# Storing the sums of a weight matrix's quarters from GpSimd's queue, every third step

## The chip, the cores and the metric

The kernel runs on one core of one Trainium2 chip. Its time is the device time of one execution in microseconds (us); a comparison uses the median of several timed runs. Traces come from one profiled execution, whose time is given beside its span. The engines are TensorE (PE, matrix products; PEld is its loading of weights), VectorE (DVE), ScalarE (ACT), GpSimd (POOL) and SyncE (SP, which here only issues DMA transfers, in the order in which they were written down). Each engine works through its own list of instructions in order, and waits where an instruction needs what another engine or a transfer has not delivered.

## The reference, cut to what matters

```
scores = matmul(q, k^T) / sqrt(64)         # 8 batches, 8 heads, 576 tokens, head of 64
keep in each row the scores that are at least its 32nd largest
attn   = softmax of what is kept;  x = matmul(attn, v), heads side by side: (8, 576, 512)
u      = x + real(fft over channels of fft over tokens of x)
un     = (u - mean(u)) / sqrt(var(u) + 1e-6)
out    = u + relu(un @ w1) @ w2            # w1: 512 x 2048, w2: 2048 x 512, all float32
```

## The kernel before

**The order of work.** All instructions are written out in the order wanted, in a loop of steps. A step `i` is one tile of 128 rows of scores (576 columns): a pair of heads has nine tiles, a batch four pairs, so a batch has 36 steps (`PER_BATCH`). In step `i` VectorE finds the 32 largest of each row of tile `i`, four rounds of MAX8 (L425) with MATCH_REPLACE8 (L427) between them, two tiles interleaved. GpSimd then scales the smallest and the largest of them (`bounds`, L434, tile `nt`). One or two steps later the tile is masked: ScalarE computes a penalty from `nt` (L448), GpSimd subtracts it from the scores (`mask`, L451, tile `wk`), ScalarE takes the exponential (L459). For most pairs from the second batch on (`by_dma`) the tile is then transposed by DMA: ScalarE copies it as two planes (L472), SP stores these (L485, L488) and reads them back transposed into `PT` (L506). TensorE multiplies `PT` with `v` (L564), computes the scores of the tile three steps ahead (L401, L386, L371), which ScalarE copies to `S` (L404, L393, L375), and in between works through a queue of units of the previous batch's two layers: the first (`hp`, L966), the second (`cp`, L993, L1032). A table `plan`, filled by `at(step, where, fn)`, holds what is issued at a fixed place of a step. The places that matter here: "pool" and "load2" both stand at the end of a step, behind that step's `bounds`, and "load2", last of all, issues transfers on SP.

**The quarters of the second layer.** From the second batch on a part of the second layer is computed with seven products of half matrices in place of eight (`fast`). It needs four sums of the quarters of `w2`, T1 to T4, which are made once. `w2` lies as 16 blocks of 128 rows; `NK` is 8, and for each `kc` of 0 to 7 the function `parts_of_w2` takes the blocks `kc` and `8 + kc`, each cut into two halves of 256 columns, and makes the four sums on GpSimd by four subtractions of 128 x 256 numbers (L923), two in a call with `half` 0 and two in the next with `half` 1. The four lie in a tile `t` of 128 x 4 x 256 numbers, 512 KB. This tile has one buffer (tag `fold_d`), so the first subtraction of the next `kc` waits until the store of the one before has landed. The store goes into the DRAM tensor `scr` (`w2_parts`; in the profile `w_parts<-w_t`, L925), each partition as four pieces of 1 KB. It is planned for "load2" of the step after the second half, on SP, in line behind everything that SP still has to issue. The program table has a quarter every two steps, from step 50 (`PER_BATCH + 14`): halves in steps 50 and 51, 52 and 53, to 64 and 65. In step 50 SP also stores two of `w2`'s quarters as they are, 1 MB each (L1379). The sums are read back by `bring` (L909) when the second batch's layers are computed.

Steps 36 to 62 are masked by way of DMA transposes, steps 63 to 71, the second batch's last pair, by TensorE (L527). Beside the quarters GpSimd has other work in these steps, two additions of the second layer's result (L1022). Behind the stage the second batch's folds (`fold_ops`) use `fold_d` again, from step 75 on.

Of the kernel before, what the change touches and what calls it, by code (L numbers as in the profile page):

```python
# [73 lines left out]
def kernel(  # L74
# [9 lines left out]
    nc = tc.nc  # L84
# [243 lines left out]
    PER_BATCH = NPB * PER_PAIR  # L328
# [574 lines left out]
    scr = dramp.tile([P, len(OPS), NK, DH], F32, name="w2_parts", tag="w2_parts")  # L903
# [9 lines left out]
    def parts_of_w2(kc, half):  # L913

        if half == 0:
            parts[kc] = batp.tile([P, 4, DH], F32, name=f"w2_t_{kc}", tag="fold_d")
        t, lo, hi = parts[kc], w2[:, kc, :], w2[:, NK + kc, :]
        sums = (
            (T1, lo[:, DH:], lo[:, 0:DH]), (T2, hi[:, DH:], t[:, T1]),
            (T3, hi[:, DH:], lo[:, DH:]), (T4, hi[:, 0:DH], t[:, T2]),  # L920
        )
        for out_, in0, in1 in sums[2 * half:2 * half + 2]:
            nc.gpsimd.tensor_tensor(out=t[:, out_], in0=in0, in1=in1, op=ALU.subtract)  # L923
        if half:
            at(now[0] + 1, "load2", lambda: nc.sync.dma_start(out=scr[:, 0:4, kc, :], in_=t))  # L925

# [377 lines left out]
    def at(step, where, fn, cost=0.0):  # L1306
        plan.setdefault((step, where), []).append(fn)
        costs[step] = costs.get(step, 0.0) + cost
# [63 lines left out]
    for kc in range(NK):  # L1372
        for half in range(2):
            at(
                PER_BATCH + 14 + 2 * kc + half, "pool",
                lambda kc=kc, half=half: parts_of_w2(kc, half),
            )
    for o, place in ((B12, w2_12), (B21, w2_21)):
        at(PER_BATCH + 14, "load2", lambda o=o, place=place: nc.sync.dma_start(  # L1379
            out=scr[:, o], in_=place  # L1380
# [65 lines left out]
    queue, waiting, pending, written, now, out_next = [], [], [], set(), [0], []  # L1446
# [227 lines left out]
```

## Time and profile before

| | us |
|---|---|
| median of 3 timed runs | 1862.91 (1859.79 to 1863.91) |
| the profiled execution | 1856.28 |
| its span, first to last instruction | 1854.5 |
| busy: PE / DVE / ACT / POOL | 1688.5 / 1584.3 / 1294.3 / 912.5 |
| mean granted clock of TensorE | 0.96 |
| the 32 sums L923 on POOL | 319.3 to 417.1 from the span's start |
| the 8 stores L925 on SP, issued | 339.2 to 417.2 |

How to read the profile: a line of a group gives engine, source line, operation, `out<-in` by the program's names, shapes and how often (x). "`A L1 <- B L2: s, n, m`" in the view of waits means that instructions of line L1 on engine A stood idle until something of L2 on B ended: s us in all, n times, m the longest. In a timeline a line gives start, duration, engine, line and operation, and in brackets the idle time just before and what ended it. The view by stretches gives, for a stretch of the span, each engine's busy time with its number of instructions (PE, PEld, DVE, ACT, POOL), the granted clock of TensorE, the DMA engines' mean busy share and GB/s. The chain is the work that ended last, each piece followed back to what released it. Issuing a transfer doesn't count as busy; SPq marks SP's issue of one.

### The profile page before, as it was taken

Reading aid. Unit: us, or ns where it says so; the run is one execution under the profiler, and the core shown is the slowest. Engines: PE = TensorE matmul, PEld = TensorE weight load, DVE = VectorE, ACT = ScalarE, POOL = GpSimd, SP = SyncE. Lnnn points to the kernel's source line nnn. Section 1 sums busy time; section 2 is a strip of 40 time slices with the busy share of each in tenths; the row PEclk is TensorE's granted clock in tenths of the full one; section 3 lists DMA queues with packets and bytes.
Section 4 is the critical chain, followed back from the end, with each engine's and each line's share of the span. In section 5 each row is a group of like instructions: output and inputs, shape, how many; then the busy total and the mean of one; then the engine's idle time right before and its main releaser. Section 6 shows DMA issues by size and latency. Waiting matters only on the chain.

```text
span 1854.5 us, 26992 instructions
## 1 busy us (share of the span) xinstructions
PE 1688.5 (91%) x8134; PEld 1082.4 (58%) x8134; DVE 1584.3 (85%) x3301; ACT 1294.3 (70%) x3104; POOL 912.5 (49%) x1278
## 2 busy tenths in 40 slices
PE   5676699789899898999999999999999999999999
PEld 3343465355465664557565665667565756686677
DVE  7999989889999999999999999999999998944010
ACT  6878658577688778878788778877887778642100
POOL 4768743454753466346543565355634654350012
PEclk8778799899999999999999999999999999999999
DMA  5333115661456954568465945586457845520051
GB/s 168 106 88 114 27 41 148 186 168 38 121 137 158 233 151 123 134 178 222 112 153 146 246 124 137 141 222 171 122 137 180 213 112 140 153 82 7 6 173 57
DMA packets 516576, 249.16 MB, mean 134 GB/s; under 512 B 398288, under 2 KB 506448, under 8 KB 516432
## 3 DMA queue, kind: packets, MB, share of 16 engines
q1 hardware_dynamic: 515664, 247.23, 51.2%
q8 instruction: 65, 1.06, 0.2%
q14 instruction: 79, 0.65, 0.1%
q10 hardware_dynamic: 768, 0.21, 0.0%
HBM read 93.63 MB, written 84.74 MB: 96 GB/s over the span
## 4 chain that ended last, share of the span: by engine, by line
PE 43%; DVE 24%; POOL 11%; ACT 9%; issue 7%; DMA 4%; SPq 1%; POOLq 0%; DVEq 0%; ACTq 0%
PE hp L966 15%; DVE wk L427 11%; DVE m L425 10%; PE o L564 5%; PE cp L993 5%; POOL wk L451 5%; PE cw L1163 4%; PE sp L401 3%; ACT wk L448 2%; PE cv L1163 2%; POOL fg L651 2%; PE yp L755 2%; ACT wk L472 1%; POOL zw L678 1%; PE cp L1032 1%
## 5 line engine op out<-in xcount | busy, mean ns | idle before, releaser
L451 POOL TENSOR_TENSOR wk<-S,wk 128x576 f32<-128x576 f32 x288 | 407.5, 1415 | 485.2 <-ACT wk L448 484.8
L425 DVE MAX8 m<-wk 128x8 f32<-128x576 f32 x864 | 626.4, 749 | 6.1
L966 PE MATMUL hp<-unT,w 128*128 128x256 f32 (+1 forms) x2048 | 526.1, 409 | 5.3 <-ACT hT L970 4.6
L966 PEld LDWEIGHTS hp<-unT,w 128*128 128x128 f32 x2048 | 380.3, 191 | 109.8 <-issue 10.4
L427 DVE MATCH_REPLACE8 wk<-m,wk 128x576 f32<-128x576 f32 x576 | 427.5, 742 | 0.0
L472 ACT COPY wk<-S 128x576 uint16<-128x576 uint16 x468 | 289.6, 670 | 0.0
L448 ACT ACTIVATE wk<-S,nt 128x576 f32<-128x576 f32 x288 | 223.4, 776 | 85.3 <-POOL nt L434 84.0
L993 PE MATMUL cp<-w,hT 128*128 128x512 f32 x512 | 234.9, 599 | 0.0
L970 ACT ACTIVATE hT<-hp 128x320 f32<-128x320 f32 (+1 forms) x256 | 103.3, 411 | 177.2 <-PE hp L966 175.6
L425 DVE MAX8 m<-S 128x8 f32<-128x576 f32 x288 | 213.7, 742 | 15.6 <-ACT S L375 15.6
L459 ACT ACTIVATE S<-wk,nt 128x576 f32<-128x576 f32 x234 | 184.2, 787 | 50.5 <-POOL wk L451 49.2
L427 DVE MATCH_REPLACE8 wk<-m,S 128x576 f32<-128x576 f32 x288 | 213.7, 742 | 0.0
L564 PE MATMUL o<-PT,v 128*64 128x256 f32 (+3 forms) x1440 | 199.3, 421 | 14.5 <-ACT x L627 5.9
L401 PE MATMUL sp<-kT,qT 64*128 64x512 f32 (+1 forms) x528 | 170.4, 673 | 12.2 <-ACT means L1357 5.7
L564 PEld LDWEIGHTS o<-PT,v 128*64 128x64 f32 x1440 | 115.7, 155 | 90.8 <-issue 22.3
L404 ACT COPY S<-sp 128x512 f32<-128x512 f32 (+1 forms) x264 | 141.8, 588 | 27.9 <-PE sp L401 26.9
L993 PEld LDWEIGHTS cp<-w,hT 128*128 128x128 f32 x512 | 93.9, 192 | 90.2 <-issue 89.3
L1108 POOL TENSOR_TENSOR hT<-hT 128x512 f32<-128x512 f32 x64 | 81.2, 1275 | 117.0 <-ACT hT L970 87.9
L434 POOL TENSOR_TENSOR nt<-m,cc 128x2 f32<-128x2 f32 x288 | 60.2, 209 | 155.4 <-DVE m L425 154.8
L1163 PE MATMUL cw<-w,hT 128*128 128x256 f32 x448 | 105.3, 385 | 12.2 <-ACT ct L1133 10.1
L371 PEld LDWEIGHTS sp_t<-kt,qT 128*128 128x128 f32 x320 | 51.0, 194 | 108.9 <-issue 67.6
L1163 PEld LDWEIGHTS cw<-w,hT 128*128 128x128 f32 x448 | 83.1, 191 | 27.9 <-ACT ct L1133 12.5
(160 smaller groups left out, 2129.6 us busy)
## 6 DMA issues: line engine op xcount, KB each, us to landing
planes<-wk SPq DMA_DIRECT2D x208, 288.0 KB, 2.7
w<-w_parts SPq DMA_DIRECT2D x82, 512.0 KB, 4.7
space<-in_moe_w_ch_dram SPq DMA_DIRECT2D x32, 512.0 KB, 3.6
nat<-in_q_dram SPq DMA_DIRECT2D x128, 64.0 KB, 2.3
v<-in_v_dram SPq DMA_DIRECT2D x64, 128.0 KB, 2.9
out_dram<-x SPq DMA_DIRECT2D x32, 256.0 KB, 2.8
nat<-in_k_dram SPq DMA_DIRECT2D x62, 128.0 KB, 3.0
planes<-wk SPq DMA_DIRECT2D x52, 144.0 KB, 2.6
```

The lines of the kernel that those rows point to most:

```text
L401: nc.tensor.matmul(sp[r], lhsT=qT[hd, q_cols], rhs=kT[hd, :], start=True, stop=True)
L404: nc.scalar.copy(out=s_t[r, keys], in_=sp[r])
L425: ops.append(lambda src=src, m8=m8: nc.vector.max(out=m8, in_=src))
L427: ops.append(lambda src=src, m8=m8: nc.vector.match_replace(w, m8, src, NEG))
L448: nc.scalar.activation(out=w, in_=Ssb[i], func=AF.Relu, scale=-FAR, bias=Nt[i][:, 1:2])
L451: nc.gpsimd.tensor_tensor(out=w, in0=Ssb[i], in1=w, op=ALU.subtract)
L459: nc.scalar.activation(out=Ssb[i] if by_dma(i) else w, in_=w, func=AF.Exp, bias=Nt.pop(i)[:, 0:1], accum_out=den_t[pair % 3][:, c:c + 1],)
L472: nc.scalar.copy(out=words[:, half, :], in_=src[:, half, :])
L564: nc.tensor.matmul(o[D * e:D * (e + 1), c0:c1], lhsT=vv[:, c, e, :], rhs=pt[:, NF if c == NF else (NF + 1) * e + c, c0:c1], start=(c == 0) ...
L966: nc.tensor.matmul(hp[:, 0:w], lhsT=w1[:, dt, P * it:P * (it + 1)], rhs=unT[:, dt, 0:w], start=(dt == 0), stop=(dt == NDT - 1),)
L993: nc.tensor.matmul(cp, lhsT=hT[:, it, P * n:P * (n + 1)], rhs=w2[:, it, :], start=(it == 0), stop=(it == NIT - 1),)
L1163: nc.tensor.matmul(dst, lhsT=h()[a][:, kc, :], rhs=rhs_of(kc), start=start and kc == 0, stop=kc == NK - 1, skip_group_check=True,)
```

## The change

Two edits. The store of a quarter is issued by GpSimd itself, right behind the four sums, in the step of the second half; it is no longer planned for the next step on SP. And a quarter is begun every third step, from step 47 on: halves in steps 47 and 48, 50 and 51, to 68 and 69.

```diff
@@ parts_of_w2
         for out_, in0, in1 in sums[2 * half:2 * half + 2]:
             nc.gpsimd.tensor_tensor(out=t[:, out_], in0=in0, in1=in1, op=ALU.subtract)
         if half:
-            at(now[0] + 1, "load2", lambda: nc.sync.dma_start(out=scr[:, 0:4, kc, :], in_=t))
+            nc.gpsimd.dma_start(out=scr[:, 0:4, kc, :], in_=t)
@@ the table of the plan
     for kc in range(NK):
         for half in range(2):
             at(
-                PER_BATCH + 14 + 2 * kc + half, "pool",
+                PER_BATCH + 11 + 3 * kc + half, "pool",
                 lambda kc=kc, half=half: parts_of_w2(kc, half),
             )
```

In the built program the lists of TensorE, VectorE and ScalarE keep their order. On GpSimd the sums stand in other places among the masks, and the eight stores follow their sums, each waiting for the last of them; the next quarter's first sum waits for the store. On SP eight transfers are gone, and the others keep their order.

## The prediction

> **What bounds the kernel now.** The page first: TensorE is busy 91% of the span and VectorE 85%, so neither bounds everywhere, and the change touches one stage only, the quarters of the second layer, which run on GpSimd from 319 to 417 us. So I read that stage by itself. The view by stretches shows it against its neighbours (the columns are busy time and instructions of each engine, granted clock, DMA share, GB/s):
>
> Ahead of the stage:
>
> ```profile
> 300.00:320.00 20.00, 17.11 (x70) 9.09 (x69) 19.76 (x42) 16.17 (x42) 7.02 (x9) 0.91 0.49 134
> ```
>
> In it and behind it:
>
> ```profile
> 340.00:360.00 20.00, 12.40 (x42) 5.38 (x39) 16.47 (x35) 10.07 (x26) 10.18 (x14) 0.74 0.65 182
> 360.00:380.00 20.00, 16.95 (x75) 6.74 (x73) 14.78 (x31) 14.95 (x39) 10.74 (x15) 0.91 0.49 147
> ...
> 420.00:440.00 20.00, 19.54 (x115) 13.10 (x113) 19.76 (x42) 15.85 (x48) 6.25 (x9) 1.00 0.14 31
> ```
>
> Before and after the stage VectorE (third busy figure) works 19.76 of 20 us: its top-k chain sets the pace, 5.09 us from one tile's first MAX8 to the next (320.60, 325.69, 330.77, 335.86). Inside the stage VectorE, TensorE and ScalarE all fall off together, and the granted clock with them. The waits of 316 to 430 us, engine by engine, say why:
>
> ```profile
> POOL w_t L923 <- DMA w_parts<-w_t: 36.4, 7, 11.0
> ```
> ```profile
> DVE m L425 <- ACT S L375: 6.6, 3, 4.3
> DVE rd L591 <- ACT rd L590: 5.4, 2, 2.9
> DVE wk L427 <- POOL w_t L923: 0.9, 1, 0.9
> DVE ct L1052 <- ACT ct L1048: 0.8, 1, 0.8
> ```
>
> GpSimd waits seven times, 36.4 us in all, for the store of the quarter before; VectorE loses 13.7 us in the same stretch, and TensorE 16.3. That the first makes the others is read from the order of work. On GpSimd:
>
> ```profile
> 332.00 0.19 POOL L434 TENSOR_TENSOR nt<-m,cc 128x2 f32<-128x2 f32 x1
> 343.17 0.72 POOL L923 TENSOR_TENSOR w_t<-w 128x256 f32<-128x256 f32 x1 [10.98 <-DMA w_parts<-w_t]
> 343.97 0.72 POOL L923 TENSOR_TENSOR w_t<-w,w_t 128x256 f32<-128x256 f32 x1
> 344.66 1.40 POOL L451 TENSOR_TENSOR wk<-S,wk 128x576 f32<-128x576 f32 x1
> ```
>
> The next tile's mask (L451) stands behind the blocked quarter. ScalarE's exponential at 346.09 has then waited 10.76 us for that mask, and the copies of the scores, which VectorE and TensorE need, stand behind it. The chain of waits of this stage runs the same way, and through SP:
>
> ```profile
> 338.58 0.59 SPq L255
> 339.18 0.04 issue
> 339.22 3.81 DMA w_parts<-w_t
> 343.08 0.09 issue
> 343.17 0.72 POOL w_t L923
> ```
>
> The first quarter's sums were done at 325.8, but its store was issued on SP at 339.22: it is queued there behind transposes, planes and the loads of v. The data then need 3.81 us (over all eight: 2.9 to 3.8). So 13.4 of 17 us were queueing.
>
> **The change, part by part.**
>
> *Removed: the place on SP.* Eight issues of 0.39 to 0.60 us go from SP, and with them the queueing. Otherwise no instruction of TensorE, VectorE or ScalarE changes its place, and SP's other transfers keep their order. On GpSimd the same 32 sums of 0.73 us (23 us) remain.
>
> *Moved: the spacing.* A quarter is made in steps 47+3k and 48+3k instead of 50+2k and 51+2k. Two whole steps, 2 x 5.09 = 10.2 us, now lie between a store's sums and the next quarter's; taking off the 1.45 us of the sums themselves, 8.7 us are left for issue and landing before GpSimd would wait. The first quarter now ends near 310 us (the L434 of step 48 stands at 308.96), ahead of the two 1 MB stores of L1379 at 322, and the last ones, in steps 65 to 69, fall where no sums were before (GpSimd is busy only 6.25 of 20 us from 420 to 440). The last store is issued in step 69; the next user of its buffer, the second batch's folds, comes from step 75. The first reading back of the parts is at 592.5 us. Both are covered.
>
> *Added: eight transfers issued by GpSimd.* The trace has none, so the time c for which one holds GpSimd is bounded by rows. Low end: SP's quickest issue of this very store, 0.39 us. High end: 4.7 us, the median landing of the 512 KB loads of L909, as if GpSimd were held until the data lay there. I take 2.0 us, the slowest issue of such a load on SP (1.99), since it is an issue and not a landing, and GpSimd has to prepare 128 x 4 pieces of 1 KB. What is queued behind it on GpSimd is the next tile's mask (L451) and, through it, ScalarE's exponential. After the undisturbed first quarter's second half GpSimd was idle 1.46 us before that mask (at 327.24). With 2.0 us in that gap the mask is late by 0.54 us, eight times: 4.3 us of lateness. The exchange rate of this stage is 13.7 us of VectorE for 36.4 of GpSimd, 0.38, so at most 1.6 us; as each lateness stands alone and the next two steps have slack, I take half, 0.8. At c = 4.7 it is 3.24 x 8 x 0.38 = 9.8 us, at 0.39 nothing.
>
> A rule speaks against the change. The rows: GpSimd's sums take 718 to 744 ns, each of the 32, with VectorE working 87% of the stage beside them; VectorE's MAX8 and MATCH_REPLACE8 don't hold GpSimd's work up. The Trainium skill, "SBUF — State Buffer", section "SBUF: two separate sides", warns that descriptors written by GpSimd starve while VectorE holds the port pair that the two share, in copies and other two-port modes. If these VectorE instructions held it, a store could wait for VectorE's gaps, and the gain would go; the rows make me think they don't. The skill's "DMA: Bandwidth & Descriptors", section "Latency and other measured facts", gives about 1 us to the first byte on GpSimd's path; with c = 1 nothing would be late and the 0.8 us would drop out.
>
> *The landing.* 2.0 + 3.8 = 5.8 us, within 8.7. Only the second quarter's store, near 326 us, meets the 1 MB stores of L1379 (4.7 and 8.5 us to land): 2.0 + 8.5 - 8.7 = 1.8 us, at 0.38 is 0.7; the next store moves half the bytes, so I take 0.4.
>
> *What is late next.* Of VectorE's 13.7 us, 0.8 (L1052) and 0.15 of L425 follow TensorE's own work: 1.0 us stays. TensorE is busy 97.75 of 114 us at a clock of 0.93, VectorE 99.18: without the stalls both need about 100, and both come out ahead by about the same, so what comes later is earlier by that amount; from 420 us both are above 19.5 of 20 busy.
>
> *Sum:* 13.7 - 1.0 - 0.8 - 0.4 = 11.5 us gained. The profiled execution took 1856.28 us (span 1854.5), so 1844.8 by its measure. It was faster than the three timed runs (1859.79 to 1863.91); against their median, 1862.91, the forecast is **1851.4**. Ends of this case: with c at 4.7, 13.7 - 1.0 - 9.8 - 0.4 = 2.5 gained, 1860.4; if TensorE's 16.3 us come back whole, because it bounds what follows, 1846.6.
>
> **Rivals.**
>
> 1. *The wait goes, and SP's and ScalarE's chain takes its place* (about 6 us gained, 1857). In this stage SP waits 12.1 us in L506 for planes to land and 23.7 in L485 for ScalarE; GpSimd's own store shares the 16 DMA engines with the transposes (share 0.6). If the transposed tiles then come late, TensorE's L564 waits and perhaps half of 11.5 is kept. Against it: at 300 to 320 us the same transposes run at VectorE's full pace, and SP loses eight issues.
>
> 2. *Slower: GpSimd becomes the bound by preparing the transfer.* Three steps last 15.3 us; GpSimd's masks and bounds take 3 x 1.60, the sums 2.92: 7.5 us are free. From c = 7.5 GpSimd sets the pace of the stage, and each store costs c - 7.5. At 7.5 + 13.7/8 = 9.2 us the gain is used up; at 11 us, 8 x 3.5 - 13.7 = 14 us are lost: 1877. [...] Against it: no row of an issue on any engine for a plain transfer exceeds 2 us.
>
> 3. *No change: the store lands too late here too.* If software's transfer through contended DMA engines takes longer than 8.7 us by the 5 us that a wait lasts now (36.4/7), the waits are back in the same place, at three steps: 1863.
>
> **How the numbers follow.** Forecast, within its ends: 0.65. Rival 1, faster too: 0.14. Rival 2: 0.14. Rival 3: 0.07. About 0.2%, 3.7 us, is what a measurement of this kernel can tell from no change; a small part of the forecast's high end falls within it, and part of rival 3 outside, so faster 0.77, same 0.08, slower 0.15. The range runs from 1846 to 1862: it holds the forecast with both ends of c, rival 1 and some of rival 3, and leaves out the slower case and what little lies below.
>
> **What would show it.** Right: no wait of L923 for w_parts, or under 3 us in all; VectorE at 19.5 of 20 in 320 to 420 us; the tile that starts its top-k at 428.13 now starts near 416; MAX8 gaps near 5.09. The distance on GpSimd from the end of a quarter's last sum to the next L451, less ScalarE's release, shows c. Wrong: that distance above 5 us with ScalarE waiting for L451 (rival 2), waits of L923 for a landing (rival 3), waits of L564 for PT (rival 1).

## The result, and the profile after

Over 22 runs each on the same chips the changed kernel takes 1854.51 us (median; 1846.04 to 1860.43), the one before 1860.36 (1856.85 to 1865.70): a ratio of 0.9967, 95% interval 0.9956 to 0.9978, so 5.9 us or 0.33% faster. Its profiled execution took 1850.13 us (span 1848.4), 6.15 less than the profiled one before. The forecast was 11.5 us; the direction and the range held, the size is about half.

The waits of 300 to 430 us in the changed kernel, on GpSimd, VectorE and TensorE:

```profile
POOL w_parts L925 <- POOL w_t L923: 2.1, 7, 0.3
```
```profile
DVE ct L1052 <- ACT ct L1048: 1.0, 1, 1.0
DVE m L425 <- ACT S L375: 0.9, 2, 0.7
```
```profile
PE o L564 <- DMA PT<-planes: 6.4, 1, 6.4
PE o L564 <- ACT x L627: 2.9, 1, 2.9
```

The 36.4 us of L923 for the store are gone, and VectorE's idle time is 1.9 us where it was 13.7. TensorE has a wait in the stage that was not there: 6.4 us for a transposed tile. Before, all of its 16.3 us were waits for ScalarE, these two among them (316 to 430 us):

```profile
PE sp_t L371 <- ACT qT L316: 5.1, 1, 5.1
PE o L564 <- ACT x L627: 3.1, 1, 3.1
```

One quarter's second half on GpSimd, with its store:

```profile
321.65 0.73 POOL L923 TENSOR_TENSOR w_t<-w 128x256 f32<-128x256 f32 x1
322.33 0.73 POOL L923 TENSOR_TENSOR w_t<-w,w_t 128x256 f32<-128x256 f32 x1
323.37 0.79 POOL L925 DMA_DIRECT2D w_parts<-w_t  x1 [0.31 <-POOL w_t L923]
324.18 1.42 POOL L451 TENSOR_TENSOR wk<-S,wk 128x576 f32<-128x576 f32 x1
```

A store holds GpSimd for 0.31 + 0.79 = 1.1 us, and here the mask follows at once. The stretches that carried the stall:

```profile
340.00:360.00 20.00, 13.57 (x48) 6.13 (x46) 19.76 (x42) 12.82 (x33) 10.59 (x14) 0.74 0.85 219
360.00:380.00 20.00, 18.39 (x87) 10.92 (x86) 18.19 (x37) 15.69 (x40) 8.26 (x11) 1.00 0.70 161
```

VectorE now works 19.76 of 20 us from 340 to 360 (16.47 before). TensorE works 13.57 us there, hardly more than the 12.40 before, and now for another reason. The chain of that stretch names it:

```profile
346.25 2.81 DMA planes<-wk
349.06 0.02 issue
349.07 4.50 DMA PT<-planes
353.57 0.25 issue
353.82 4.53 PE o L564 x20
```

and SP's issues show why the planes set out only at 346:

```profile
318.32 1.05 SPq L1379 DMA_DIRECT2D w_parts<-w  x2
319.41 8.24 SPq L506 DMA_TRANSPOSE PT<-planes  x1
327.77 1.23 SPq L488 DMA_DIRECT2D planes<-wk  x2
331.26 1.30 SPq L506 DMA_TRANSPOSE PT<-planes  x1
```

The transpose behind the two 1 MB stores of L1379 takes 8.24 us to be issued, where the others from there to 370 us take 1.3 to 4.0; everything on SP comes later from there.

**Where the time went.** Instructions of VectorE keep their order, so one and the same can be compared: its lead is how much earlier it starts than in the first profile before. Leads in us, worked out from the traces, at MAX8 of a tile; "stage" is the difference between tiles 40 and 88, "behind" between 88 and the last:

```
                                tile 40   tile 88   tile 287   stage   behind
changed kernel                     2.7      13.9       7.1      11.2     -6.8
changed kernel, again (e4)         1.2       8.5      -0.3       7.3     -8.9
spacing alone (e1)                 0.2      11.0       9.1      10.8     -1.9
SP, three steps, same step (e8)    0.2      11.0       4.5      10.8     -6.5
queue alone (e2)                   1.8       9.2       9.7       7.4      0.5
late copies alone (e7)             2.8       6.6       2.4       3.9     -4.2
both edits, late copies (e3)       1.6      19.2      13.9      17.6     -5.4
the same again (e12)               1.8      19.4      10.9      17.6     -8.5
spacing, SP, late copies (e6)      1.2      18.8      19.3      17.6      0.5
the same again (e11)               0.8      18.3      12.5      17.5     -5.8
before, again (e5)                 0.3       0.2       1.0       0.0      0.7
```

So the stage gave what was forecast in one profile and less in the other (2.7 and 1.2 us of lead were there ahead of it, where the two programs don't differ), and then some 7 to 9 us were given back in the 1100 us from there to the last tile, where no instruction differs either. One program's stage varies as well: e10 below, which is the kernel before up to tile 90, took 6.0 us longer in it than the first profile before. Two questions for the runs: what each edit does, and where the second half went.

### The profile page after: what moved, and what is told of

It reads as the page before. It is cut to its first block, busy times and chain, and to the rows that moved or that the text cites. A ratio compares the mean times of both kernels' runs of the same rounds, so it can differ in the third digit from the quotient of the medians.

```text
span 1848.4 us, 26992 instructions
## 1 busy us (share of the span) xinstructions
PE 1686.1 (91%) x8134; PEld 1084.1 (59%) x8134; DVE 1581.0 (86%) x3301; ACT 1294.9 (70%) x3104; POOL 919.5 (50%) x1286
## 3 DMA queue, kind: packets, MB, share of 16 engines
q1 hardware_dynamic: 511440, 243.04, 51.2%
q0 software_dynamic: 1152, 4.19, 0.7%
## 4 chain that ended last, share of the span: by engine, by line
PE 45%; DVE 27%; POOL 9%; issue 8%; ACT 7%; DMA 3%; SPq 0%; POOLq 0%; DVEq 0%; ACTq 0%
PE hp L966 16%; DVE wk L427 12%; DVE m L425 12%; PE cp L993 5%; PE o L564 5%; POOL wk L451 4%; PE sp L401 3%; PE cw L1163 3%; PE cv L1163 2%; ACT wk L448 2%; PE yp L755 2%; POOL fg L651 2%; PE cp L1032 2%; PE mp L816 1%; PE sp_t L371 1%
## 5 line engine op out<-in xcount | busy, mean ns | idle before, releaser
L425 DVE MAX8 m<-S 128x8 f32<-128x576 f32 x288 | 213.7, 742 | 10.3 <-ACT S L375 10.2
L564 PE MATMUL o<-PT,v 128*64 128x256 f32 (+3 forms) x1440 | 198.7, 421 | 22.0 <-DMA PT<-planes 13.0
L401 PE MATMUL sp<-kT,qT 64*128 64x512 f32 (+1 forms) x528 | 168.9, 669 | 9.3 <-ACT means L1357 5.7
L564 PEld LDWEIGHTS o<-PT,v 128*64 128x64 f32 x1440 | 116.0, 155 | 97.8 <-issue 34.5
L1163 PE MATMUL cw<-w,hT 128*128 128x256 f32 x448 | 104.9, 384 | 12.6 <-ACT ct L1133 10.2
```

The costliest lines, as they stand in the source:

```text
L401: nc.tensor.matmul(sp[r], lhsT=qT[hd, q_cols], rhs=kT[hd, :], start=True, stop=True)
L425: ops.append(lambda src=src, m8=m8: nc.vector.max(out=m8, in_=src))
L564: nc.tensor.matmul(o[D * e:D * (e + 1), c0:c1], lhsT=vv[:, c, e, :], rhs=pt[:, NF if c == NF else (NF + 1) * e + c, c0:c1], start=(c == 0) ...
L1163: nc.tensor.matmul(dst, lhsT=h()[a][:, kc, :], rhs=rhs_of(kc), start=start and kc == 0, stop=kc == NK - 1, skip_group_check=True,)
```

## The experiments

Each kernel was timed beside the kernel before on the same chip; that one's median was 1857.79 us for e1 to e4, 1858.65 for e5 to e8 and 1864.88 for e9 to e12.

**Spacing alone (e1).** The store goes back to SP, the three steps stay.

```diff
-            nc.gpsimd.dma_start(out=scr[:, 0:4, kc, :], in_=t)
+            at(now[0] + 1, "load2", lambda: nc.sync.dma_start(out=scr[:, 0:4, kc, :], in_=t))
```

> Spacing alone: quarters every third step from step 47, the stores still on SP in the step behind the second half. Theory A (GpSimd's wait for the landing held the masks, and both edits are needed to end it): SP's line still delays stores, one step of 5.1 us is left for issue and landing (3.4 us when nothing stands ahead), so the waits of L923 fall from 36.4 us to 8 to 20 us, and 2 to 4 us of the total are gained. Rival B (the longer spacing does all, and GpSimd's own queue brings nothing or costs): waits under 5 us and a gain of 6 us or more, as with both edits.

1844.97 against 1857.79 us, ratio 0.9925 (0.9902 to 0.9949): more than both edits. The waits of L923 are as theory A had them, 10.2 us, but nearly all in one, behind the 1 MB stores:

```profile
POOL w_t L923 <- DMA w_parts<-w_t: 10.2, 2, 8.6
```

The long wait leaves VectorE 0.9 us idle and TensorE 5.1 (L401, waiting for ScalarE's copies). Theory A is right on the waits and wrong on the time, rival B the other way round: the spacing does most, although a wait of GpSimd is left.

**Queue alone (e2).** GpSimd's own queue with quarters every second step from 50.

```diff
-                PER_BATCH + 11 + 3 * kc + half, "pool",
+                PER_BATCH + 14 + 2 * kc + half, "pool",
```

> Queue alone: the store issued by GpSimd behind the sums, quarters every second step from step 50 as before. Theory A: 5.1 us of a step less 1.45 us of sums leave 3.6 us for 1.1 us of issue and 4.4 us of landing, so each of seven waits is about 2 us, 10 to 18 us in all; at 0.38 that leaves VectorE 4 to 7 us of idle time, and 3 to 5 us of the total are gained. Rival B: transfers of GpSimd's queue disturb SP's transposes, waits of L564 for PT grow, no gain (within 2 us of the kernel before).

1849.45 us, ratio 0.9951 (0.9931 to 0.9970); waits of L923 8.1 us in five, less than expected. Either edit alone takes away most of the 36.4 us, and the two don't add up. L564 waits 6.8 us for PT at the same place as with both. Rival B foresaw that wait, but the gain of 8.3 us is above what either theory gave.

**The 1 MB stores out of the way (e3, e12).** Both edits, and L1379 at step 66.

```diff
-        at(PER_BATCH + 14, "load2", lambda o=o, place=place: nc.sync.dma_start(
+        at(PER_BATCH + 30, "load2", lambda o=o, place=place: nc.sync.dma_start(
```

> Both edits, and the two 1 MB stores of L1379 moved from step 50 to step 66, where the DMA engines are nearly idle (share 0.15 to 0.21). Theory A, second part: the 6.4 us in which L564 waits for PT near 350 us come from SP's line, which falls behind when the transpose after the two stores takes 8.2 us to issue; without them that wait is under 2 us and 3 to 6 us more are gained, 1849 to 1852 on the scale of 1860.4 before. Rival B: the wait for PT comes from GpSimd's stores on the same DMA engines, stays at 5 us or more, and the total is that of both edits.

1844.74 us, ratio 0.9926 (0.9909 to 0.9943). The wait of L564 for PT in the stage is gone from the list (in e12 1.9 us are left, for planes), the slowest transpose lands in 5.9 us instead of 11.3, and the lead from the stage rises to 17.6 us. That settles the 6.4 us: they were SP's line behind L1379. Beside the changed kernel on the same chip (e4) the time is 10.5 us less, more than the 3 to 6 expected.

**The changed kernel again (e4).**

> The changed kernel once more, for a second profile. What is lost behind the stage (9.6 us of lead between steps 76 and 288 in the first pair of profiles): if it is chance of single transfers, this profile shows its losses at other places and of another size, with a lead of 10 to 14 us at step 76 as before; if it comes from the change, the losses near steps 84, 150, 184 and 256 come again at the same sizes.

1855.19 us, ratio 0.9979 (0.9968 to 0.9989). Its profiled execution (1858.06) has the wait for PT at the same place, 7.0 us, and a second way in which late transfers reach VectorE:

```profile
DVE wk L427 <- DMA planes<-wk: 4.5, 1, 4.5
```

Its size is about the 3.9 us by which the stage is worth less than in the first profile. Behind the stage it loses 2.6 us near tile 148 (the first profile 2.8) and 4.5 near 256 (2.8): the same places, partly other sizes, so neither of the two answers is clear from this pair.

**The kernel before again (e5).**

> The kernel before once more, for a second profile. Its first profiled execution (1856.28 us) lay 2 to 4 us under its median. If the losses behind the stage that all other profiles show against it (near steps 84 and 148) are that execution's good luck, this profile shows them too: 2 us each, and a time of 1857 to 1862; if they come from the edits, it doesn't.

1858.88 us, ratio 1.0001 (0.9991 to 1.0012). Its profile follows the first one within 0.6 us up to tile 184 and within 1.5 to the end, and loses nothing near 84 and 148. So their absence is not the good luck of one execution. The loss near 84 is not the edits' alone, though: e10, which is the kernel before up to tile 90, has it too (2.1 us between tiles 80 and 88). Beside e10 it comes, with 1.8 to 2.0 us, in the edited kernels that have L1379 at step 50 (the changed kernel, e4, e1, e8, e2), and is 0.2 us or less in all with L1379 at step 66. The one near 148 occurs, with 1.1 to 2.9 us, in all ten profiles of the edited kernels e1 to e4, e6 to e8, e11, e12 and the changed kernel itself.

**SP, three steps, late copies (e6, e11).** e1 with the edit of e3.

> Spacing alone with the stores on SP, and the two 1 MB stores moved to step 66. Theory now (the spacing ends GpSimd's wait; SP's line behind the 1 MB stores is the second cause; GpSimd's own queue costs): the one wait of 8.6 us that spacing alone left, behind the 1 MB stores, goes, and with it 3 to 5 us: 1840 to 1842 on the scale of 1857.8 before. Rival (the late copies give the same with either queue): the time of both edits with late copies, 1845.

1837.63 us (1837.52 to 1839.51), ratio 0.9893 (0.9878 to 0.9907). Waits of TensorE in the stage:

```profile
PE o L564 <- ACT x L627: 4.8, 2, 2.9
PE hp L966 <- ACT hT L970: 1.6, 1, 1.6
PE sp L401 <- ACT S L375: 1.0, 1, 1.0
PE sp_t L371 <- ACT PT L530: 0.5, 1, 0.5
```

None is for a transfer, and both engines run through the stretch with little idle time, by the view by stretches:

```profile
340.00:360.00 20.00, 18.14 (x89) 7.99 (x87) 19.78 (x41) 17.57 (x48) 11.18 (x15) 1.00 0.77 201
360.00:380.00 20.00, 18.38 (x85) 11.55 (x82) 19.81 (x40) 16.19 (x39) 8.77 (x11) 1.00 0.77 174
```

TensorE's 18.14 stand against 13.57 of the changed kernel and 12.40 before; the granted clock is 1.00 instead of 0.74. This beats both kernels of the change.

**Late copies alone (e7).** The kernel before with the edit of e3.

> The kernel before with only the two 1 MB stores moved to step 66. If SP's line behind them is what made GpSimd's waits long, the waits fall from 36.4 us to 15 to 25 (the first, 11 us, and part of the others go), and 4 to 7 us are gained; if spacing is what counts, waits stay above 28 us and under 3 us are gained.

1856.24 us, ratio 0.9992 (0.9978 to 1.0006): no difference that can be told. The waits of L923 are 28.5 us, the longest 6.4 instead of 11.0. Most of the 36.4 us was the spacing, not the 1 MB stores; these count only once the spacing is right.

**Stores on SP, as early as on GpSimd (e8).** e1 with the store in the step of the second half.

```diff
-            at(now[0] + 1, "load2", lambda: nc.sync.dma_start(out=scr[:, 0:4, kc, :], in_=t))
+            at(now[0], "load2", lambda: nc.sync.dma_start(out=scr[:, 0:4, kc, :], in_=t))
```

> Spacing of three steps, the store on SP but in the step of the second half itself, as early as on GpSimd's queue; the 1 MB stores at step 50. It takes the queue apart from the time of issue. If GpSimd's queue costs because its transfers run beside the transposes, this gains as much as spacing alone (12 to 14 us) or 1 to 2 us more, as its waits of L923 fall under 9 us; if issuing a step earlier is what costs (SP's planes and transposes come later behind the store), it gains only what both edits do, 4 to 6 us.

1847.34 us, ratio 0.9949 (0.9929 to 0.9968): between the two cases named, so it doesn't decide between queue and time of issue. Waits of L923 3.5 us, and TensorE's wait is there without any transfer of GpSimd's:

```profile
PE o L564 <- DMA PT<-planes: 5.9, 1, 5.9
```

So the wait for PT is not made by GpSimd's queue. Whoever frees GpSimd of its stall brings TensorE to that tile before SP has it.

**The same work at another moment (e9, e10).** Ten more MAX8, 7.4 us on VectorE, at tile 90, in e6 and in the kernel before. They repeat one that is there, so nothing else is computed.

```diff
-            ops.append(lambda src=src, m8=m8: nc.vector.max(out=m8, in_=src))
+            for _ in range(11 if (i, r) == (90, 0) else 1):
+                ops.append(lambda src=src, m8=m8: nc.vector.max(out=m8, in_=src))
```

> The version with the stores on SP, three steps, and the 1 MB stores at step 66, with ten more MAX8 (0.74 us each, repeating one that is there) on VectorE at step 90, behind the stage: 7.4 us later in time and nothing else. It asks whether what the profiles lose behind the stage (0 to 10 us, at waits of L564 for PT) depends on the moment at which the same work runs. If it does, this version, which lost 0.1 us there, loses some at steps 144 to 264 and its time is more than 7.4 us above 1837.6 (1847 to 1853); if it doesn't, 1845 and no more.

> The kernel before with the same ten MAX8 at step 90. Both its profiles agree to 0.3 us up to step 176. If the moment counts, the profile shows other losses or gains behind step 90 than 7.4 us, 1 to 3 us near step 148 as the edited kernels have it; if not, the lead against the kernel before is -7.4 us from step 90 to the end, and the time 1866.

e9: 1853.65 us, beside 1843.36 of the same version without the delay (e11, same chip), 10.3 more. e10: 1873.10 beside 1864.88, ratio 1.0039 (1.0023 to 1.0055), 8.2 more. From tile 88 to 96 both profiles fall back by 7.9 us. Behind it e9 loses 5.0 us near tile 148, where e6 lost 2.5 and e11 1.1; e10 loses 2.1 there, where the kernel before lost nothing in two profiles. The delayed kernel before, 846 to 905 us, shows the wait that the edited kernels show there (its lines stand one further down, L565 is L564):

```profile
PE o L565 <- DMA PT<-planes: 2.0, 1, 2.0
```

So that loss needs no store of GpSimd's, and in this profile no edit but a delay of VectorE. The times say less: 8.2 us (interval 4.3 to 10.3) can't be told from the 7.4 of the ten MAX8, and e10's profile wins back most of its 2.1 us further on. These are single profiles, and e10's had lost 6.0 us against the first one before between tiles 40 and 88, ahead of the ten MAX8.

**The two queues side by side (e11, e12).** e6 and e3 once more.

> Stores on SP, three steps, 1 MB stores at step 66, once more and with more rounds, beside the same with GpSimd's queue. If GpSimd's queue costs even where the 1 MB stores are out of the way, this is 4 to 8 us faster than that; if the difference seen (7 us of medians of four runs) was chance, the two are within 2 us.

> Both edits with the 1 MB stores at step 66, once more with more rounds: 1842 to 1846 if GpSimd's queue costs, as against 1837 to 1840 with SP's; within 2 us of that if not. In the stage itself both had the same lead, 17.6 us, so a cost would have to show behind step 88.

SP's queue: 1843.36 us (1839.73 to 1844.71), ratio 0.9873 (0.9855 to 0.9892). GpSimd's: 1846.85 (1840.87 to 1854.02), 0.9900 (0.9878 to 0.9922). The intervals overlap here; in the earlier pair they did not (0.9878 to 0.9907 against 0.9909 to 0.9943), and with L1379 at its old place e1 and e4 were 10.2 us apart. In each of the three pairs SP's queue is ahead, by 3.5 to 10 us. In all three SP's store is also planned one step later than GpSimd's, so queue and time of issue go together in them.

## Why the prediction was right in direction and half wrong in size

**The bound.** Right. Once the stores no longer block GpSimd, VectorE's idle time goes from 13.7 to 1.9 us and its pace is 5.09 us a tile.

**The issue on GpSimd.** Taken at 2.0 us, it was 1.1; the masks behind the stores start at once or wait for ScalarE. The Trainium skill's "DMA: Bandwidth & Descriptors", section "Latency and other measured facts", gives about 1 us to the first byte on this path. The 1.1 us that GpSimd was held are near it, but are another quantity: no trace here shows the first byte. The rule against the change, of VectorE starving GpSimd's descriptors, did not show: seven stores of 786 ns and one of 961, beside a VectorE that works 91 to 99% of each 20 us. The slower rival is refuted for this size: it needed 7.5 us.

**The landing.** Taken at 3.8 us, it was 4.4 in the median, 3.4 to 7.1 (9.7 in e4), the long one beside L1379 as foreseen; in the first profile no wait came of it, in e4 one of 0.5 us. Why it is 1.0 us above the 3.4 of SP's stores before is not told apart.

**What is late next.** This step failed. It said that TensorE and VectorE "both come out ahead by about the same, so what comes later is earlier by that amount". TensorE came out with 6.4 to 7.0 us of waiting for PT, where the forecast had none; it is rival 1, taken as an alternative to the forecast though it happened on top of it. The evidence against it, that at 300 to 320 us the same transposes keep pace, was read from a stretch that lies ahead of L1379. The trace before had the cause in plain sight:

```profile
322.36 1.19 SPq L1379 DMA_DIRECT2D w_parts<-w  x2
323.59 7.76 SPq L506 DMA_TRANSPOSE PT<-planes  x1
```

The kernel before only hid it, since GpSimd's stall of 11 us held TensorE back in the same place. e3 and e6 price it: with L1379 at step 66 the stage is worth 17.6 us, with it at step 50 7 to 11. VectorE pays behind the window that the forecast looked at. From 430 to 520 us it is idle 7.4 us before, 8.7 in the changed kernel and 4.4 in e3; in this order, its waits for TensorE's transposes:

```profile
DVE x L608 <- PE tpx L604: 4.4, 2, 2.7
DVE x L608 <- PE tpx L604: 4.1, 2, 2.5
DVE x L608 <- PE tpx L604: 1.6, 1, 1.6
```

With the 1.9 us up to 430 (none in e3) the changed kernel's VectorE is idle 6.2 us longer than e3's, which is the difference of the two stages, 6.4 us.

That the first profile's stage came out at 11.2 us, close to the 11.5, is therefore partly luck. The forecast left out the wait for PT, and it also left out that VectorE's idle time behind 430 us could shrink. It had read that from 420 us both engines are above 19.5 of 20 busy; that holds to 440 us, but from there the view before has:

```profile
440.00:460.00 20.00, 17.73 (x81) 9.97 (x78) 18.58 (x39) 13.82 (x41) 8.62 (x19) 0.91 0.07 15
460.00:480.00 20.00, 18.12 (x51) 7.76 (x49) 17.86 (x37) 13.43 (x31) 15.53 (x21) 1.00 0.34 95
```

Rival 1's 6 us are close to the 5.9 measured, and that too is partly luck: in the first profile the stage kept 11.2 us in spite of the wait, and what is missing from the total went behind it.

**The sum.** That a lead from one stage stays to the end was taken for granted. It did not: from tile 88 on the changed kernel gives back 6.8 and 8.9 us in its profiles, and in the first one this is most of what separates the 11.2 us of the stage from the result. From tile 96 to the last L564 waits 6.6 and 10.9 us for PT (3.7 and 2.0 in the two profiles before), and VectorE is idle 42.6 and 44.5 us (35.6 and 34.5), the largest part of it in L608, for TensorE (19.2 and 20.2 us; before 15.4 and 15.8). What is shown: the loss near tile 148 comes in edited kernels with either queue, and, in one profile, in the kernel before with VectorE delayed by 7.9 us. What is not settled: why the versions with the stores on SP are faster by 3.5 to 10 us although their lead from the stage is the same (10.8 against 11.2 and 7.3; 17.5 and 17.6 against 17.6). The difference lies behind the stage, where the programs don't differ, and profiles of one kernel differ there by 6 us (e6 and e11). Whether it is the moment again, the step in which the store is issued, or something that GpSimd's queue leaves behind was not told apart; e2, with that queue, lost nothing there.

**A hypothesis for GpSimd's transfers in the stage.** With them the slowest transpose, the one behind L1379, lands in 11.0 to 11.9 us (changed kernel, e2, e4), with SP's stores in 9.1 to 10.0 (e1, e5, e8, the kernel before, e10). The page of the changed kernel has the queues:

```profile
q1 hardware_dynamic: 511440, 243.04, 51.2%
q0 software_dynamic: 1152, 4.19, 0.7%
```

GpSimd's stores go in packets of 3.6 KB on average (4.19 MB in 1152), SP's queue averages 475 bytes; the same stores on SP are 4224 packets of 1 KB (515664 before less 511440). The skill's section "Queues, rings and completion order" of the same page says that an engine takes turns between queues packet by packet; if so, a large packet takes more of each turn from the transposes. No run changed the packets, so this is argued, not shown, and it has a plain rival: GpSimd's store of 512 KB goes out at 323.4 to 325.8 us, in the middle of that transpose, SP's next one at 332.3 at the earliest, when the transpose has all but landed. More bytes at the same time could cost as much.

## What to carry to other kernels

A wait that is removed shows the next one only on the path that the wait had kept late: look in the old trace for the slow transfer just behind the stall (here an issue of 7.8 us), and price it on top of the forecast, not instead of it. To space a single-buffered store further apart can be worth more than a faster or private queue: three steps alone on SP's queue gave 0.75%, both edits 0.2 to 0.3%. Large copies that nobody needs soon belong where the DMA engines are idle: moving two 1 MB stores gave nothing alone, and brought the spaced version from 0.75% to 1.07 and 1.27%.

## What was unexpected of the hardware

All versions run the same instructions from tile 96 on. From tile 96 to 144, 258 us, all profiles but one (e1, 1.1 us) agree to 0.1 us, and there are single places at which they part by 1 to 5 us (tile 148, and in some 190, 224 and 256); in e10, with VectorE delayed by 7.9 us ahead of it, tile 148 came out as in the edited kernels.
